# Fused attention and two feed-forward layers on one Trainium2 core: raw weights in ten places, 64x32 head tiles, a new layout of the first pass

## The chip, the cores and the metric

The kernel runs on one core of one Trainium2 chip. The metric is the device time of one execution in microseconds: the median of 3 runs is 771.13 us (770.52 to 771.54).

## The reference

```python
# attention: x is (4, 8, 512, 64), state is (4, 8, 32, 64), per batch and head, scale 1/8
a = softmax(scale * x @ state.T);      xread = a @ state      # rows of x read the state
a2 = softmax(scale * state @ x.T);     sread = a2 @ x         # the state reads x
t = concatenate([xread, sread], axis=2)    # then heads side by side: (2176, 512) tokens
h = t @ w_in                               # moe: 512 -> 2048
g = where(h >= 1, h, where(h <= -1, 0, (h + 1) ** 2 / 4))
t = g @ w_out                              # 2048 -> 512
h = t @ w_in2;  g = softplus(h);  out = g @ w_out2            # moe2, the same sizes
```

The weights are 64-bit floats; x, state and the output are 32-bit floats.

## The kernel before, in words

There are two phases. Phase 1 does attention and the first feed-forward layer for four tiles of 512 tokens (one batch each, the x tokens) and a small tile `s` of the 128 state tokens; phase 2 does the second layer over five tiles of 512 or 384 tokens. A tile is worked off in windows (16 of them, 4 for `s`), each for 128 of the 2048 hidden columns: 132 windows in all, in the loop `for i in range(NW + LAG + 1)`. In window `i` PE issues the first-layer products of window `i` (`l1`, 6 in phase 1) and the second-layer products of window `i - LAG` (`l2`, 12 in phase 1, three per block, as each operand is split into a high and a low fp32r part: `mm3`). Between them ACT opens the activation (`act_open`), DVE closes it (`close`), ACT copies the high part (`cut_hi`), and DVE (POOL in tile 0) subtracts the low part (`cut_lo`).

In phase 1 the read of the state is folded into the weights: for each batch `b` and pair `p` of 128-column blocks, `g_mm` (L404) multiplies the batch's state by the rebuilt weights `W1[p]` in four fp32 products of 256 columns. The stationary operand is `stb`, 64 columns wide, in which the two heads of a product stand block by block between zeros. `g_split` cuts the result into `gh` and `gl`; `l1` multiplies them by the transposed attention weights `ahi`, `alo`. `scores` (L213) uses `stb` in the same way with 512 columns of x. `Attn` holds the attention of one batch: names with `s_` belong to the softmax over x (its result `x1s` goes to tile `s`), names with `n_` to the softmax over the 32 states. `hops()` is a generator that does a few of these steps per window; `rest()` does the `s_` steps of batch 0 later.

The weights come as 64-bit floats (`w.bitcast(U32)`, two words each). A `Pair` is 1 MB of them: `load` issues the DMA on SP's queue into one of two buffers `ws`, `scale` (ACT, L107) and `conv` (DVE, L123 and L124) rebuild a 32-bit float, and `split` copies the high part (ACT) and subtracts the low part (POOL, L70, `wl<-cv,wh`). `pairs` is sorted by the window in which a pair is rebuilt; a load is issued when the pair two before it has been rebuilt, a `scale` one window ahead.

All instructions stand in the order in which the code issues them (`manual_schedule`): every engine works off its own queue in order, and so does SP with its DMAs. Ahead of the loop stands the start: state, pair 0 and x of batch 0 are loaded, x is transposed (L198), and the `n_` steps of batch 0 run through DVE and ACT until the first `l1` can go.

Of the kernel before, what the change touches and what calls it, by code (L numbers as in the profile page):

```python
# [18 lines left out]
def fused_kernel(ctx: ExitStack, tc: tile.TileContext, x, state, w1, w2, w3, w4, out):  # L19
# [10 lines left out]
    P = 128  # L30
# [12 lines left out]
    LAG = 3  # L43
    C2 = 2 * P
# [20 lines left out]

    def copy(dst, src):
        nc.scalar.activation(dst, src, AF.Copy)  # L67
# [7 lines left out]
    M = 2  # L75

# [3 lines left out]
    class Pair:  # L80
        def __init__(self, w, inward, p, dst, slots=None):
            self.w, self.inward, self.p, self.dst, self.slots = w, inward, p, dst, slots

        def load(self, tag=None, eng=None):
# [8 lines left out]
            if tag is None:  # L93
                self.raw = [new(base, shape, U32, "ws", 2)]
                nc.sync.dma_start(self.raw[0], src)
                return
            self.raw = [new(base, [P, 512 * M], U32, tag, 8) for _ in range(2)]
# [28 lines left out]
        def split(self):  # L126
# [3 lines left out]
            hi, lo = (new(pool, [P, 1024], F32R, t, n) for t in ("wh", "wl"))  # L130
            copy(hi, self.v)
            sub(nc.gpsimd, lo, self.v, f32(hi))
# [15 lines left out]
    stb = new(p1, [P, NJ, B, 2 * N], F32, "stb")  # L148
    nc.gpsimd.memset(stb, 0.0)
# [6 lines left out]
    def load_x(b, engs):  # L156
        xt[b] = new(at, [P, R, H, D], F32, f"x{(b + 1) // 2 % 2}")
        src = x[b].rearrange("h (p r) d -> r p h d", r=R)
        for r in range(R):
            engs[r % len(engs)].dma_start(xt[b][:, r], src[r])  # L160

    def warm(n):

        t = bank("l1", 2)
        for _ in range(n):
            nc.tensor.matmul(t[:, :P], ident, ident, start=True, stop=True)

    def load_state():
        st = new(at, [P, H, D], F32, "xT0")
        for b in range(B):  # L170
            eng = (nc.sync, nc.scalar)[b % 2]
            eng.dma_start(st[b * N : (b + 1) * N], state[b].rearrange("h n d -> n h d"))
        return st

    def place_state(st):
        ps = bank("at", 2).rearrange("p (j c) -> p j c", j=NJ)
        for j in range(NJ):
            nc.tensor.transpose(ps[:, j, :], st[:, 2 * j : 2 * j + 2, :].rearrange("p e d -> p (e d)"), ident)
        for e in range(2):
            sl = slice(e * D, (e + 1) * D)  # L180
            nc.vector.tensor_copy(
                stb[sl, :, :, e * N : (e + 1) * N], ps[sl].rearrange("p j (b n) -> p j b n", n=N)
            )
# [5 lines left out]
    class Attn:  # L189
# [6 lines left out]
        def x_transpose(self, j, ps, r):  # L196
            xb = xt[self.b]
            nc.tensor.transpose(  # L198
                ps[:, r * P : (r + 1) * P], xb[:, r, 2 * j : 2 * j + 2, :].rearrange("p e d -> p (e d)"), ident
            )  # L200
# [8 lines left out]
        def scores(self, g):  # L209
            self.ps[g] = bank("at", 2)  # L210
            for i in range(2):
                j = 2 * g + i
                nc.tensor.matmul(  # L213
                    self.ps[g][64 * i : 64 * i + 64, :], stb[:, j, self.b, :], self.xT[j], start=True, stop=True
                )

        def s_copy(self, g):
            self.e2[g] = new(base, [P, S], F32, "xs", 4) if self.b == 0 else new(at, [P, S], F32, f"xT{2 * g}")
            copy(self.e2[g], self.ps[g])

        def blocks(self, g, src=None):

            self.st[g] = new(at, [P, S], F32, "sa", 3)
            nc.vector.transpose(self.st[g], self.e2[g] if src is None else src)
# [17 lines left out]
        def s_turn(self, g):  # L242
            self.ps[g] = bank("at", 2)
# [13 lines left out]
        def s_read(self, js):  # L257
            xb = xt[self.b]
            if 0 in js:
                self.ps["s"] = bank("at", 2)  # L260
            for j in js:
                for r in range(R):
                    for e in range(2):
                        c0 = (2 * (j % 2) + e) * N
# [3 lines left out]
                            self.a2T[j // 2][:, r, c0 : c0 + N],  # L268
# [38 lines left out]
        def hops(self):  # L307

            for js in ((0, 1), (2,), (3,)):
                ps = [bank("at", 2) for _ in js]  # L310
                for j, t in zip(js, ps):
                    for r in range(R):
                        self.x_transpose(j, t, r)
                yield
                for j, t in zip(js, ps):
                    self.x_copy(j, t)
                yield
            self.scores(0)
            yield
            self.s_copy(0)  # L320
            yield
            self.scores(1)
            yield
            self.s_copy(1)
            self.blocks(0)
            self.s_max(0)
            yield
            yield
            self.s_exp(0)
            self.s_max(1)  # L330
            self.n_sub(0)
            self.blocks(1)
            yield
            yield
            self.s_exp(1)
            self.n_exp(0)
            self.s_norm(0)
            self.n_sub(1)
            yield
            self.s_turn(0)  # L340
            yield
            self.s_keep(0)
            self.s_norm(1)
            self.n_exp(1)
            self.n_norm(0)
            yield
            self.s_turn(1)
            yield
            self.s_keep(1)
            self.n_norm(1)  # L350
            self.n_back(0)
            yield
            self.s_read((0, 1))
            yield
            self.n_hi(0)
            if self.b < 3:
                self.n_lo(0)
            self.n_back(1)
            yield
            self.s_read((2, 3))  # L360
            yield
            self.n_hi(1)
            for g in range(NG):
                if self.b < 3 and g == 1 or self.b == 3 and g == 0:
                    self.n_lo(g)
            self.s_out()
            yield
            if self.b == 3:
                yield
                self.n_lo(1)  # L370
                yield

        def rest(self):
            yield
            for g in range(NG):
                self.s_max(g)
            yield
            yield
            for g in range(NG):
                self.s_exp(g)  # L380
            yield
            yield
            for g in range(NG):
                self.s_norm(g)
            yield
            for g in range(NG):
                self.s_turn(g)
                yield
                self.s_keep(g)
                yield  # L390
            self.s_read((0, 1, 2, 3))
            yield
            self.s_out()
            yield
# [11 lines left out]
    def g_split(b, p, ps):  # L406
        hi = new(p1, [P, NG * C2], F32R, "gh", 2)
        lo = new(p1, [P, NG * C2], F32R, "gl", 2)
        copy(hi, ps)
        sub(nc.vector, lo, ps, f32(hi))  # L410
        G[b, p] = [t.rearrange("p (g f) -> p g f", g=NG) for t in (hi, lo)]
# [14 lines left out]
    tiles2 = [units[0:4], units[4:8], units[8:11], units[11:14], units[16:17] + units[14:16]]  # L426
# [54 lines left out]
    def l1(w):  # L481
# [13 lines left out]
        elif w.ph == 1:  # L495
# [3 lines left out]
            terms = [(gh, ah, g) for g in range(NG)] + [(gh, al, g) for g in range(NG)] + [(gl, ah, g) for g in range(NG)]  # L499
# [31 lines left out]
    def evac(w):  # L531
        if w.ph == 1 and w.tl == "s":
# [3 lines left out]
            def pe():  # L536
                ps = bank("at", 2)
# [13 lines left out]
        for i in range(n):  # L551
            t = new(base, [P, 512], F32, "xs", 4)
            if i % 2 == 0:
# [54 lines left out]
    pairs = []  # L608
# [4 lines left out]
    for p in range(1, NP):  # L613
        plan_pair(Pair(w1, True, p, W1), 2 * (p - 1))
    for p in range(NP):
        plan_pair(Pair(w2, False, p, W2, lambda: pools["b"]), 2 * p + 1)
# [5 lines left out]
    pairs.sort(key=lambda t: t[0])  # L622
    for n, (a, pair) in enumerate(pairs):
        if n >= 3:
            b = pairs[n - 2][0]
            when(b + (b >= A0), "load", pair.load)
        if n >= 1:
            when(a - 1, "late", pair.scale)
        n = 2 if a >= A0 else 1
        for k in range(n):  # L630
# [3 lines left out]
    def plan_g(i, b, p):  # L634
        def pe():
            ps = bank("at", 2)
            g_mm(b, p, ps)
            return lambda: g_split(b, p, ps)
# [3 lines left out]
    for b, t0 in ((0, 0), (1, NF), (2, 2 * NF), (3, T3)):  # L642
        for p in range(NP):
            if (b, p) != (0, 0):
                plan_g(t0 + 2 * p - (1 if b == 0 else 2), b, p)
    gens = {}

    def plan_hops(i, make):


        def start():
            gens[i] = make()
# [3 lines left out]
    for b, i0, i1 in ((1, -1, 4), (2, NF - 1, NF + 5), (3, 2 * NF - 1, 2 * NF + 1)):  # L656
        when(i0, "load", lambda b=b: load_x(b, [nc.sync]))
        plan_hops(i1, lambda b=b: Attn(b).hops())
# [19 lines left out]
    with tc.manual_schedule():  # L678
# [106 lines left out]
```

## Time and profile before

| | us |
|---|---|
| median of 3 runs | 771.13 |
| the profiled execution | 772.06 |
| its span | 770.2 |
| PE busy | 743.0 (96%) |
| ACT busy | 458.3 (60%) |
| DVE busy | 437.3 (57%) |
| POOL busy | 103.7 (13%) |

The profile shows one execution. Busy times are sums over the span; a matmul's record lasts longer than its share of PE, since matmuls overlap, so the time from one start to the next is what it costs. A row's bracket says how long the engine sat idle ahead of it and what ended that. PEclk is the granted clock of TensorE as a share of 2.4 GHz.

### The profile page before, as it was taken

How to read it: one execution, taken by the hardware profiler on the slowest of the kernel's cores; microseconds unless marked ns; L12 is line 12 of the kernel's file. 1: busy time of each engine (PE TensorE's matmuls, PEld its weight loads, DVE VectorE, ACT ScalarE, POOL GpSimd, SP SyncE). 2: the span in 40 equal slices, each digit the busy share in tenths (PEclk: the TensorE clock that was granted, in tenths of full speed). 3: DMA queues.
4: the chain of work that ended last, by engine and by line, in shares of the span. 5: the costliest groups of instructions: out<-in, count | busy, mean ns of one | idle time of the engine just before them, and what ended most of it. 6: DMA issues, size and time to landing. Idle time of an engine off the chain costs nothing.

```text
span 770.2 us, 9775 instructions
## 1 busy us (share of the span) xinstructions
PE 743.0 (96%) x3768; PEld 606.3 (79%) x3768; DVE 437.3 (57%) x695; ACT 458.3 (60%) x800; POOL 103.7 (13%) x60
## 2 busy tenths in 40 slices
PE   5599899999999999999999999999999999999997
PEld 4366677867767788777888888888889998998986
DVE  4877964245337424555599984554654554555543
ACT  3677675445545435566778775655655666566563
POOL 0265670002000001122222320000000000000000
PEclk9799999999999999999999999999999999999999
DMA  9466363300010003144343400300020002001001
GB/s 289 110 217 217 109 194 81 55 1 1 1 55 1 1 1 110 56 128 159 110 164 110 164 0 1 96 1 1 0 89 9 1 0 83 1 1 41 1 1 41
DMA packets 39582, 52.00 MB, mean 68 GB/s; under 512 B 19312, under 2 KB 21872, under 8 KB 39536
## 3 DMA queue, kind: packets, MB, share of 16 engines
q1 hardware_dynamic: 36912, 50.73, 21.1%
q10 hardware_dynamic: 2624, 0.66, 0.4%
q8 instruction: 29, 0.48, 0.3%
q14 instruction: 17, 0.14, 0.1%
HBM read 42.47 MB, written 8.91 MB: 67 GB/s over the span
## 4 chain that ended last, share of the span: by engine, by line
PE 92%; DVE 4%; ACT 2%; DMA 1%; POOL 1%; issue 0%; SPq 0%; DVEq 0%; ACTq 0%
PE acc L441 16%; PE acc L442 16%; PE acc L443 16%; PE l L501 10%; PE l L443 8%; PE l L441 8%; PE l L442 8%; PE at L404 4%; PE l L488 2%; PE at L265 1%; PE at L213 1%; DMA wh<-in_moe_w_in_dram 1%; DVE w L124 1%; PE at L198 1%; DVE w L123 1%; POOL wl L70 0%
## 5 line engine op out<-in xcount | busy, mean ns | idle before, releaser
L70 DVE TENSOR_TENSOR gtl<-tl,gth 128x384 fp32r<-128x384 f32 (+1 forms) x80 | 48.9, 611 | 148.6 <-ACT gth L67 148.6
L577 ACT ACTIVATE ta<-l 128x384 f32<-128x384 f32 (+1 forms) x80 | 42.8, 535 | 128.7 <-PE l L443 128.7
L573 ACT ACTIVATE ta<-l 128x512 f32<-128x512 f32 x68 | 40.6, 598 | 128.2 <-PE l L501 104.3
L70 DVE TENSOR_TENSOR gtl<-ta,gth 128x512 fp32r<-128x512 f32 x52 | 36.0, 692 | 136.6 <-ACT gth L67 136.6
L442 PE MATMUL acc<-wl,gth 128*128 128x512 f32 x288 | 113.3, 393 | 0.0
L441 PE MATMUL acc<-wh,gth 128*128 128x512 f32 x288 | 113.2, 393 | 0.0
L443 PE MATMUL acc<-wh,gtl 128*128 128x512 f32 x288 | 112.7, 391 | 0.0
L441 PE MATMUL acc<-gth,wh 128*128 128x512 f32 x256 | 104.7, 409 | 0.0
L443 PE MATMUL acc<-gth,wl 128*128 128x512 f32 x256 | 100.2, 391 | 0.4 <-POOL wl L70 0.4
L442 PE MATMUL acc<-gtl,wh 128*128 128x512 f32 x256 | 100.3, 392 | 0.0
L70 POOL TENSOR_TENSOR wl<-cv,wh 128x1024 fp32r<-128x1024 f32 x24 | 62.8, 2615 | 220.8 <-ACT wh L67 219.5
L443 PE MATMUL l<-x,wl 128*128 128x384 f32 (+1 forms) x192 | 68.7, 358 | 0.0
L441 PE MATMUL l<-x,wh 128*128 128x384 f32 (+1 forms) x192 | 68.6, 357 | 0.0
L442 PE MATMUL l<-x,wh 128*128 128x384 f32 (+1 forms) x192 | 68.5, 357 | 0.0
L443 PEld LDWEIGHTS acc<-wh,gtl 128*128 128x128 f32 x288 | 54.1, 188 | 12.2
L441 PEld LDWEIGHTS acc<-gth,wh 128*128 128x128 f32 x256 | 48.1, 188 | 19.1 <-issue 9.1
L441 PEld LDWEIGHTS acc<-wh,gth 128*128 128x128 f32 x288 | 54.1, 188 | 11.2 <-issue 0.8
L442 PEld LDWEIGHTS acc<-wl,gth 128*128 128x128 f32 x288 | 54.0, 188 | 10.0
L443 PEld LDWEIGHTS acc<-gth,wl 128*128 128x128 f32 x256 | 48.1, 188 | 11.6 <-POOL wl L70 0.8
L70 DVE TENSOR_TENSOR tl<-tl,ta 128x384 f32<-128x384 f32 (+1 forms) x80 | 55.3, 691 | 2.8
L588 DVE SCALAR_TENSOR_TENSOR ta<-tb,ta 128x384 f32<-128x384 f32 (+1 forms) x80 | 55.9, 698 | 0.0
L442 PEld LDWEIGHTS acc<-gtl,wh 128*128 128x128 f32 x256 | 48.2, 188 | 8.8
(114 smaller groups left out, 1376.2 us busy)
## 6 DMA issues: line engine op xcount, KB each, us to landing
ws<-in_moe_w_out_dram SPq DMA_DIRECT2D x16, 1024.0 KB, 4.8
ws<-in_moe_w_in_dram SPq DMA_DIRECT2D x14, 1024.0 KB, 5.5
xd<-xs SPq DMA_DIRECT2D x16, 256.0 KB, 2.9
out_dram<-xs SPq DMA_DIRECT2D x16, 256.0 KB, 2.5
x<-in_x_dram SPq DMA_DIRECT2D x14, 256.0 KB, 6.2
xs<-xd SPq DMA_DIRECT2D x8, 256.0 KB, 6.3
wh<-in_moe_w_in_dram SPq DMA_DIRECT2D x2, 512.0 KB, 5.5
wl<-in_moe_w_in_dram SPq DMA_DIRECT2D x2, 512.0 KB, 7.7
```

The lines of the kernel that those rows point to most:

```text
L70: eng.tensor_tensor(dst, a, b, op=ALU.subtract)
L123: nc.vector.tensor_scalar(d, lo, 29, None, op0=ALU.logical_shift_right)
L124: nc.vector.scalar_tensor_tensor(d, hi, 3, d, op0=ALU.logical_shift_left, op1=ALU.bitwise_or)
L404: nc.tensor.matmul(o, stb[:, j, b, :], W1[p][:, j, :], start=True, stop=True)
L441: nc.tensor.matmul(o, lh, rh, start=first, stop=False)
L442: nc.tensor.matmul(o, lh, rl, start=False, stop=False)
L443: nc.tensor.matmul(o, ll, rh, start=False, stop=last)
L488: nc.tensor.matmul(w.h[:, i * P : (i + 1) * P], W1[f // 2][:, k, (f % 2) * P : (f % 2 + 1) * P], x1s[:, k, :], start=(k == 0), stop=(k == ...
L501: nc.tensor.matmul(w.h, l[:, g, f], r[:, g, :], start=i == 0, stop=i == len(terms) - 1)
L573: nc.scalar.activation(w.a, w.hc, AF.Relu, bias=1.0)
L577: nc.scalar.activation(w.a, w.hc, AF.Abs)
L588: nc.vector.scalar_tensor_tensor(w.a, w.b, 1.0, w.a, op0=ALU.subtract, op1=ALU.subtract)
```

## The change

- `stb` (zeros between the heads) goes; `stT` holds the transposed state without zeros, `stT0` that of batch 0. `heads` does `g_mm` and `scores` in eight products of 64 rows by 32 columns of the array, the two row halves into two PSUM banks of one lasting tile `side`, which also takes the place of the two rotating banks `at`. For batch 0, `scores0` does 16 products of 256 columns.
- The x of batch 0 is loaded in rows of 1 KB, in two DMAs on SP's queue behind pair 0; the state of batch 0 comes by itself, by ACT's queue, that of all batches later.
- The first ten pairs are loaded at once: besides the two buffers `ws`, the eight places of the split second-layer weights `wh0` to `wl7` take raw weights until their own are split. `A1` and `A2` say in which window a pair is rebuilt.
- The start also rebuilds pairs 1 of `w1` and 0 of `w2`, does `g_mm` of pair 1, and issues warm-up products between the steps.
- In the loop the order of the steps is a list (`ORDER`: windows 0 to 2, 3 to 15, the rest); `l2` follows two windows behind until window 14, three after. Attention of batch 1 does only its `n_` steps in tile 0, its `s_` steps (`rest`) start in window 17.
- The low parts of the weights and of tile 0's activations are subtracted by DVE instead of POOL. The order of the three terms in `l1` changes, the state tokens' tile stands elsewhere in `tiles2`, and the last output block is copied and stored in two halves.

```diff
+    LEAD = 14
+    ORDER = [
+        "l1 post hops evac open close l2 split early conv hi late hops lo pe load".split(),
+        "l1 post hops evac close l2 split early open conv hi late hops lo pe load".split(),
+        "l1 hops evac post close l2 split early hops open hi conv pe lo late load".split(),
+    ]
+    side = new(psum, [P, 2, 512], F32, "at")
...
             copy(hi, self.v)
-            sub(nc.gpsimd, lo, self.v, f32(hi))
+            sub(nc.vector, lo, self.v, f32(hi))
...
+    def scores0(xT):
...
+        for j in range(NJ):
+            for e in range(2):
+                for q in range(2):
...
+                    nc.tensor.matmul(
+                        side[j * N : (j + 1) * N, q, c], stT0[rows, h * N : (h + 1) * N], xT[j][rows, c], start=True, stop=True
+                    )
+    def heads(b, o, rhs):
+        for j in range(NJ):
+            for e in range(2):
+                rows = slice(e * D, (e + 1) * D)
+                if b == 0:
+                    s_h = stT0[rows, (2 * j + e) * N : (2 * j + e + 1) * N]
+                else:
+                    s_h = stT[rows, j, b * N : (b + 1) * N]
+                nc.tensor.matmul(o(e)[j * N : (j + 1) * N, :], s_h, rhs(j)[rows], start=True, stop=True)
...
-    def g_mm(b, p, ps):
-        for j in range(NJ):
-            i = j % 2
-            o = ps.rearrange("p (g f) -> p g f", g=NG)[64 * i : 64 * i + 64, j // 2, :]
-            nc.tensor.matmul(o, stb[:, j, b, :], W1[p][:, j, :], start=True, stop=True)
+    def g_mm(b, p, two=None):
+        o = (lambda e: side[:, e, :C2]) if two is None else (lambda e: two[e][:, :C2])
+        heads(b, o, lambda j: W1[p][:, j, :])
...
-            w.lo = nc.gpsimd if tl == 0 else nc.vector
+            w.lo = nc.vector
...
+    A1 = [-3, -2, 1, 3, 6, 6, 8, 12]
+    A2 = [-1, 2, 4, 4, 8, 10, 13, 15]
...
+    room = [(-9, None), (-9, None)] + [(-9, p) for p in range(NP)]
...
+    when(1, "pe", lambda: place_state(st))
+    when(1, "pe", lambda: warm(8))
+    for b, i0, i1 in ((1, -1, 3), (2, NF + 3, NF + 6), (3, 2 * NF - 1, 2 * NF + 1)):
         when(i0, "load", lambda b=b: load_x(b, [nc.sync]))
-        plan_hops(i1, lambda b=b: Attn(b).hops())
+        plan_hops(i1, lambda b=b: attn(b).head(), lambda b=b: aT0[b].reads(b > 1))
+    plan_hops(NF + 1, lambda: aT0[1].rest())
...
+        early[0].load()
+        load_x(0, [nc.sync])
+        for pair in early[1:3]:
+            pair.load()
         st = load_state()
+        for pair in early[3:]:
+            pair.load()
         warm(8)
+        place_state0(st0)
+        warm(8)
...
+        a0.scores()
+        warm(30)
+        run(-2, "early")
+        run(-2, "conv")
         for g in range(NG):
             a0.blocks(g, a0.ps[g])
...
+            k = i - LAG + (i < LEAD)
+            u = wins[k] if 0 <= k < NW and i != LEAD else None
```

## Rows read from the trace of the kernel before

**Rows 1.** The page, engines: busy us (share of the span) xinstructions.
```profile
PE 743.0 (96%) x3768; PEld 606.3 (79%) x3768; DVE 437.3 (57%) x695; ACT 458.3 (60%) x800; POOL 103.7 (13%) x60
```

**Rows 2.** Table by stretch: stretch, length, busy us of each engine, clock, DMA.
```profile
0.00:24.82 24.82, 10.79 (x53) 7.95 (x53) 13.43 (x24) 8.50 (x13) 2.64 (x8) 0.84 0.99 264
24.82:43.36 18.54, 13.78 (x52) 8.90 (x53) 14.35 (x18) 12.05 (x19) 6.89 (x4) 0.84 0.38 117
43.36:75.78 32.42, 32.42 (x157) 23.63 (x157) 24.62 (x28) 25.30 (x38) 19.13 (x10) 1.00 0.64 224
75.78:110.95 35.17, 31.81 (x206) 24.57 (x205) 31.74 (x42) 24.19 (x40) 24.32 (x15) 1.00 0.39 124
110.95:765.19 654.24, 654.20 (x3305) 541.23 (x3303) 353.20 (x588) 387.67 (x692) 50.72 (x25) 1.00 0.15 47
765.19:770.20 5.01, 0.00 (x0) 0.00 (x0) 0.01 (x1) 0.60 (x1) 0.00 (x0) 0.78 0.49 157
```

**Rows 3.** PE's timeline at the first windows: start us, us, operation [idle before <-releaser].
```profile
24.82 0.80 PE L501 MATMUL l<-ahi,gh 128*128 128x512 f32 x1 [8.02 <-ACT ahi L67]
...
43.36 0.73 PE L501 MATMUL l<-ahi,gh 128*128 128x512 f32 x2 [1.44 <-ACT gh L67]
```

**Rows 4.** PE's timeline around products with the state and of tile `s`.
```profile
112.40 1.08 PE L404 MATMUL at<-w,stb 128*64 128x256 f32 x8
113.41 0.50 PE L441 MATMUL acc<-gth,wh 128*128 128x512 f32 x1
...
160.78 1.08 PE L213 MATMUL at<-xT,stb 128*64 128x512 f32 x4
...
283.98 3.73 PE L488 MATMUL l<-x1s,w 128*128 128x128 f32 x32
287.47 0.48 PE L441 MATMUL acc<-gth,wh 128*128 128x512 f32 x1
```

**Rows 5.** All records of line 404 behind the first: count, min/median/max ns.
```profile
L404 PE MATMUL at<-w,stb x248: 379/379/431, 31.4 to 363.4; 128*64 128x256 f32 x124
```

**Rows 6.** Table by stretch, two of the loads' early stretches; last number GB/s.
```profile
12.00:14.00 2.00, 2.00 (x12) 2.00 (x12) 0.53 (x1) 0.00 (x0) 0.00 (x0) 0.58 1.08 399
...
22.00:24.00 2.00, 0.00 (x0) 0.00 (x0) 1.90 (x5) 0.38 (x1) 0.00 (x0) 0.50 1.11 180
```

**Rows 7.** DVE's timeline: start of the chain, a rebuilding, two long ones.
```profile
15.98 0.72 DVE L224 STREAM_TRANSPOSE sa<-at 128x512 f32<-128x512 f32 x1 [0.57 <-PE at L213]
...
27.41 0.42 DVE L123 TENSOR_SCALAR w<-wl 128x512 uint32<-128x512 uint32 x1
27.87 0.69 DVE L124 SCALAR_TENSOR_TENSOR w<-wl,w 128x512 uint32<-128x512 uint32 x1
28.48 0.42 DVE L123 TENSOR_SCALAR w<-wl 128x512 uint32<-128x512 uint32 x1
...
59.44 2.12 DVE L124 SCALAR_TENSOR_TENSOR cv<-ws,cv 128x1024 uint32<-128x1024 uint32 x1
...
70.53 1.22 DVE L124 SCALAR_TENSOR_TENSOR cv<-ws,cv 128x1024 uint32<-128x1024 uint32 x1
```

**Rows 8.** The chain that ended last, in order of time: start us, us, what.
```profile
127.63 0.44 PE at L245 x4
...
133.21 1.84 PE at L265 x64
...
139.36 0.87 PE at L198 x8
...
170.18 1.36 PE l L501 x6
...
174.25 1.36 PE l L501 x6
```

**Rows 9.** Groups by line and shape: busy us, mean ns, idle before.
```profile
L70 POOL TENSOR_TENSOR wl<-cv,wh 128x1024 fp32r<-128x1024 f32 x24 | 62.8, 2615 | 220.8 <-ACT wh L67 219.5 <-PE at L198 1.3
```

**Rows 10.** Timeline of the last copy.
```profile
765.19 0.60 ACT L67 ACTIVATE xs<-acc 128x512 f32<-128x512 f32 x1 [0.76 <-PE acc L443]
```

More of the change, by code (lines that the diff above doesn't have):

```diff
@@ L75, in fused_kernel @@
     M = 2
+    halves = [0]
     def flat(t):
@@ new lines, in scores0, with warm2 @@
+    def scores0(xT):
+        for j in range(NJ):
+            for e in range(2):
+                for q in range(2):
+                    rows = slice(q * D, (q + 1) * D)
+                    h = 2 * j + e
+                    c = slice(e * 256, (e + 1) * 256)
+                    nc.tensor.matmul(
+                        side[j * N : (j + 1) * N, q, c], stT0[rows, h * N : (h + 1) * N], xT[j][rows, c], start=True, stop=True
+                    )
+    def warm2(n):
+        for _ in range(n):
+            nc.tensor.matmul(side[:, 0, :P], ident, ident, start=True, stop=True)
@@ L305, in n_lo @@
             sub(eng or self.eng, self.alo[:, g, :], self.st[g], f32(self.ahi[:, g, :]))
[L307 to L371, printed above, removed]
@@ L373, in rest, with x_turn @@
-        def rest(self):
[L374 to L394, printed above, removed]
+        def x_turn(self, js):
+            for j in js:
+                self.ps["x", j] = at_bank()
+                for r in range(R):
+                    self.x_transpose(j, self.ps["x", j], r)
@@ L397, in fused_kernel, with both @@
+        def rest(self):
+            def both(f):
+                return lambda: [f(g) for g in range(NG)]
+            yield None, both(self.s_max)
+            yield None, both(self.s_exp)
+            yield None, both(self.s_norm)
+            yield both(self.s_turn), both(self.s_keep)
+            yield self.s_read, self.s_out
     W1 = [None] * NP
     G = {}
-    def g_mm(b, p, ps):
-        for j in range(NJ):
-            i = j % 2
-            o = ps.rearrange("p (g f) -> p g f", g=NG)[64 * i : 64 * i + 64, j // 2, :]
-            nc.tensor.matmul(o, stb[:, j, b, :], W1[p][:, j, :], start=True, stop=True)
@@ L414, in fused_kernel, with g_split @@
+    def g_split(b, p):
+        hi, lo = g_tiles(b, p)
+        copy(hi, side[:, :, :C2])
+        sub(nc.vector, lo, side[:, :, :C2], f32(hi))
     class Win:
@@ L552, in evac @@
             t = new(base, [P, 512], F32, "xs", 4)
+            if w is wins[-1] and i == n - 1:
+                b, r = tiles2[w.tl][i]
+                o = out[b * T : b * T + S, :].rearrange("(p r) d -> p r d", r=R)[:, r, :]
+                for c, eng in ((slice(0, 256), nc.sync), (slice(256, 512), nc.scalar)):
+                    if c.start:
+                        copy(t[:, c], acc[i][:, c])
+                    else:
+                        nc.vector.tensor_copy(t[:, c], acc[i][:, c])
+                    eng.dma_start(o[:, c], t[:, c])
+                break
             if i % 2 == 0:
@@ L709, in fused_kernel @@
             a0.n_exp(g)
-        early[0].scale()
+        g_mm(0, 1)
+        hi, lo = g_tiles(0, 1)
+        warm(14)
+        copy(hi, side[:, :, :C2])
         for g in range(NG):
-            a0.n_norm(g, nc.vector)
+            a0.n_norm(g, (nc.vector, nc.gpsimd)[g])
+        sub(nc.vector, lo, side[:, :, :C2], f32(hi))
         for g in range(NG):
@@ L715, in fused_kernel @@
             a0.n_hi(g)
+        for g in range(NG):
             a0.n_lo(g, nc.vector)
-        plan_hops(NF - 1, a0.rest)
+        run(-1, "early")
+        run(-1, "conv")
         run(-1, "load")
```

290 lines of the change are left out of this document (177 added, 113 removed).

## The prediction

> **What bounds the kernel now.** First the page's line of engines [rows 1]: PE is busy 96% of the span, DVE 57%, ACT 60%. That is a mean over unlike stretches, so next the table by stretch [rows 2]. From 110.95 us to the last matmul PE has 654.20 us of work in 654.24 us: there only a change in PE's own work moves the end. Before that it is another kernel. The first first-layer product starts at 24.82; from there to 43.36 PE works 13.78 of 18.54 us, from 75.78 to 110.95 31.81 of 35.17. Third, PE's timeline [rows 3]: the first product waited 8.02 us for ACT's `ahi`, and the one at 43.36 waited for `gh`, which ACT copies out of a product that needs a weight pair rebuilt on DVE. Fourth, DVE in those stretches [rows 2]: 31.74 busy of 35.17. So the start is bounded by DVE, everything after by PE. The waits there are DVE's time, not the ACT's that they name.
>
> I measure by one mark: the start of the seventeenth `l1`, the first of tile 1, at 110.95 us [rows 2].
>
> **The change, part by part.**
>
> *Small head tiles.* `g_mm` was four fp32 products of 256 columns, 128 rows by 64 columns of the array, half of the state operand zeros. It becomes eight of 64 by 32. First what one product costs: an fp32 product is two records, and 16 full-array products of 128 columns take 283.98 to 287.47 = 3.49 us, 0.218 each [rows 4]; 256 columns would be 0.436. Four in turn would be 1.74 us, but the block takes 112.40 to 113.41 = 1.01 us [rows 4], and two 512-column products (0.87 each) take 1.08 us with their end. So two products on different column halves run fully beside each other, both passes of each. If eight small tiles do the same, `g_mm` is one step of 0.44 us, plus what is over today: 1.01 - 2 x 0.436 = 0.14. Taken: 0.59, a saving of 0.42. No row shows 64-row tiles or more than two products side by side. From below the block can't go under 0.44; from above, eight in turn would be 3.5. If they overlap only in pairs, 4 x 0.436 + 0.14 = 1.88, a loss of 0.87; in fours, 1.01, no change. I take eight because what the rows show for two tiles (each tile goes on by itself, with its second pass not holding up the next tile's first) holds for eight if tiles are independent. There are 31 blocks behind the first (248 records, 8 to a block [rows 5]), of which 23 stand behind the mark (seven of batch 1, eight each of batches 2 and 3): 23 x 0.42 = 9.7 us, all on PE's path. `scores` of batches 2 and 3: two blocks of 1.0 us become one of 0.87 + 0.14; about 0.95 less each, 1.9 us.
>
> The Trainium skill, "TensorE: Matmul & The Clock Gate", Part 3 (the mechanism), says matmuls keep strict program order in start and end; the two passes of one product would then hold up the next tile, and eight products would be some nine half steps, about 2 us. The two-tile rows speak against it: in strict order two 512-column products need three steps of 0.436 = 1.31 us, and 1.08 was measured. "TensorEngine Tiling (Array Packing)", Key Properties, says the reverse, that tiles run independently; by that the block is the 0.59 above.
>
> *Start, up to the first product.* Removed: the zero fill of `stb`, x in small pieces on two queues. Added ahead of the first product: the state of batch 0 by itself, warm-up products, rebuilding of pair 1 (DVE) and `g_mm`/`g_split` of pair 1. Weights and x in large rows came at 399 GB/s, in 256-byte rows at 180 [rows 6]. x of batch 0 now comes in 1 KB rows right behind one weight pair: 2.2 MB from an assumed 2 us on, estimated at 300 to 400 GB/s, is there by 8 to 9.5 us. But ahead of the softmax chain DVE now has pair 1: two halves of 0.42 + 0.69 [rows 7], at their pitch (27.41 to 28.48) 1.07 each, 2.1 us. Walking the queues: pair 0 rebuilt by 8.8, products and transposes to 13, copies to 13.6, pair 1 on DVE to 16.6. So the chain starts near 16.5, against 15.98 [rows 7]. The chain itself (15.98 to 24.82) keeps its length: some 0.7 for `g_split`'s subtraction comes in, one multiplication goes to POOL. First product: 25.3, against 24.82; bounds 22 (DVE's pair 1 fits into the wait for the scores) and 28 (it doesn't fit, and x is late). No gain here, but pair 1 and its G are done, so that windows 0 to 3 have their operands.
>
> *First pass.* What is in it for PE in 16 windows: 16 `l1` of 1.36 and 13 `l2` of 2.71 (window 174.25 - 170.18 = 4.07 less 1.36) [rows 8]: 57.0. Further 7 g blocks of 0.65 with the change of mode (4.6), x transposes (16 in two steps of 0.87 [rows 8] with the change of tile, 2.0), scores of batch 1 (1.1), state (0.5): 65. Before, 8 blocks at 1.1, scores 2.1, turns of `e2` 2 x 0.44 and `s_read` 1.84 + 0.2 [rows 8] were in it too: 73, and 110.95 - 24.82 = 86.1 passed; 13 us were stalls and slow products.
> DVE: 13 pairs at 2.1 (27), 7 subtractions of 1024 columns now here instead of on POOL (L124's 1.22 of the same size [rows 7]: 8.5), 16 `close` and 16 `cut_lo` at the pitch of a 512-column instruction, 27.87 to 28.48 = 0.6 [rows 7] (19), 7 `g_split` (4.2), batch 1's column softmax (6), state (0.6): 66 us. Before it was busy 14.35 + 24.62 + 31.74 = 70.7 [rows 2], with `s_max`, `s_norm` in it. The move from POOL costs DVE some 18 us in this pass (8.5 + 16 x 0.6) and takes away the cause of its long instructions: L124 of 1024 columns took 2.12 at 59.44, a time in which POOL subtracted, and 1.22 at 70.53 with POOL idle [rows 7]; POOL's own subtraction took 2.6 in the mean [rows 9], twice as long.
> So PE has 65 and DVE 66, and what is left are waits between them. I walked windows 0 to 16 in ORDER's queue order: the first `l2` starts at 34.5 (waits for `cut_lo`, which waits for DVE's pairs 2 and 1 of the two weights), windows 4 and 9 lose 1.6 and 0.8 us, and the mark falls at 97.5. I add 1 us for hand-overs: 98.5; that leaves PE stalls of about 8. Bounds: 93 (stalls of 2.5) and 107 (the 13 us as before). Gain 12.4.
> What hides the rest: loads. Ten pairs and x are queued at once, 12.4 MB; at 399 GB/s they are there at 34, x of batch 1 (1 MB at 180 to 220) behind them at 39 to 40. It is needed at window 3's transposes, 39.3. If the mean is 300 GB/s, x is there at 50, and PE, which takes its work in order, stands 10 us with `l2` queued behind.
>
> *Moved.* `s_turn` and `s_read` of batch 1 (0.9 + 2.0) now stand behind the mark where PE is full: -2.9. Their DVE and ACT work goes to a stretch where DVE is busy 353 of 654 us.
>
> *POOL's later `wl` on DVE.* 17 subtractions of 1.2 behind the mark. Between weights and second layer DVE is fullest, but loses the same contention; PE has run 100% there. Taken 0, bound +3.
>
> *End.* The last copy (0.60 on ACT) and its store are halved over two engines and queues; from 765.19 to 770.2 it is 5.0 us [rows 10]. Taken -0.5, bounds 0 and -1.
>
> Sum: 12.4 - 2.9 + 9.7 + 1.9 + 0.5 = 21.6. The profiled execution: 772.06 with 770.2 of span; 750.5 after. The median of the runs, 771.13, lies 0.9 below: 749.6, said 750.
>
> **Rivals.**
> *A. Heads in fours.* No gain from tiles: 9.7 + 1.9 back, and some 1 us in the first pass: 763. For it: no row shows more than two. Against it: the two-tile rows show no sharing at all.
> *B. Order holds the tiles up (slower).* Only pairs overlap: each block 0.87 dearer, each `scores` 1.7 (8 x 0.436 + 0.14 = 3.6 against 2.0). Behind the mark 23 x 0.87 + 2 x 1.7 = 23.4; in the first pass 7 x 0.87 + 1.7 = 7.8, which eats the gain of 12.4 to 4.6. 771.1 - 4.6 + 2.9 + 23.4 - 0.5 = 792. It decides from about 1.34 us for a block on: without the heads the rest gives 12.4 - 2.9 + 0.5 = 10.0, which 30 blocks use up at 0.33 each.
> *C. The first pass stays bound.* Heads as forecast, but x of batch 1 comes late, or DVE's rebuilding in bursts (two pairs in windows 4, 6 and 8, 4.3 us each beside PE's 4.7) keeps the stalls: mark at 107, 758. For it: DVE at 66 against 65. Against it: loads had 399 GB/s where nothing held them.
> *D. It does more than that:* the mark at 93 and scores in one step: 744.
>
> **How the numbers follow.** Forecast 0.58 (744 to 756 with D's side in it), A 0.12, C 0.18, B 0.12. A and C are faster too. A measurement here tells 0.2%, 1.5 us, from no change. Faster 0.86, same 0.02 (only a mixture of B and the first pass's gain lands there), slower 0.12. The range leaves out B and a thin lower tail: 740 to 767.
>
> **What would show it.** Right: the rows of `g_mm` as 16 records within 0.55 to 0.7 us up to the next product, 23 of them behind the mark; the seventeenth `l1` near 98; no POOL beside L124, and L124 at its short length; PE without idle time from the mark on; clock 1.00 from 20 to 30 us, where the rows show 0.50 at 22 (1.2 of 2.4 GHz) after PE had stood for most of 8 us [rows 3, 6]. Wrong: blocks of over 1 us (A), of near 2 (B), a wait of the transposes for x, or of `l2` for `cut_lo` in windows 4 to 10 (C).

## The result, and the profile after

The changed kernel takes 753.5 us (median; 752.58 to 754.91) against 771.16 of the kernel before in the same session: ratio 0.9773 [0.9756 to 0.979]. The forecast was 750, with 740 to 767 as range. The profiled execution has 753.69 us and a span of 751.7 (772.06 and 770.2 before).

The page's line of engines, as in [rows 1]:

```profile
PE 742.1 (99%) x4216; PEld 610.2 (81%) x4216; DVE 442.9 (59%) x758; ACT 460.2 (61%) x811; POOL 17.6 (2%) x20
```

PE's busy time is nearly what it was; its idle time has fallen from 27.2 to 9.6 us, and POOL does next to nothing. The table by stretch, cut at the first first-layer product and at the mark, answers to [rows 2] (stretch, length, busy us of PE, PEld, DVE, ACT, POOL, clock, DMA, GB/s):

```profile
0.00:28.23 28.23, 25.30 (x225) 22.80 (x225) 14.63 (x30) 9.10 (x15) 2.79 (x8) 1.00 0.98 345
28.23:60.00 31.77, 29.59 (x179) 21.81 (x179) 28.83 (x48) 27.37 (x45) 0.00 (x0) 1.00 0.75 236
60.00:100.47 40.47, 40.47 (x239) 30.13 (x239) 37.08 (x60) 31.04 (x52) 7.63 (x6) 1.00 0.22 79
100.47:747.00 646.53, 645.99 (x3575) 535.26 (x3574) 361.30 (x621) 392.32 (x700) 7.22 (x6) 1.00 0.15 48
```

From 60 us to the last product PE is idle for 0.5 us only; before, its last stalls lay between 80 and 100 us. The mark lies at 100.47 (forecast 98.5, before 110.95): 10.5 us are won ahead of it, and 8.0 behind it (751.7 - 100.47 = 651.2 against 770.2 - 110.95 = 659.25). The first product comes at 28.23, *later* than before (24.82) and than the forecast (25.3).

PE's timeline of the changed kernel (start us, us, operation [idle before <-releaser]): the start, and blocks with the state:

```profile
6.71 1.03 PE L207 MATMUL at<-ident,cv 32*128 32x32 f32 x8 [1.57 <-DMA cv<-in_state_dram]
7.67 3.62 PE L195 MATMUL acc<-ident 128*128 128x128 f32 x16
11.23 0.66 PE L250 MATMUL l<-w,stT 64*32 64x256 f32 x16
11.82 2.05 PE L226 MATMUL at<-ident 128*128 128x128 f32 x16
13.71 1.91 PE L270 MATMUL acc<-ident,x 128*128 128x128 f32 x16
...
28.22 0.50 PE L546 MATMUL l<-ahi,gh 128*128 128x512 f32 x1
...
32.15 1.95 PE L195 MATMUL acc<-ident 128*128 128x128 f32 x16
...
37.85 0.50 PE L487 MATMUL acc<-gtl,wh 128*128 128x512 f32 x1 [0.98 <-DVE gtl L84]
...
40.58 0.66 PE L250 MATMUL at<-w,stT 64*32 64x256 f32 x16
41.17 0.74 PE L546 MATMUL l<-ahi,gh 128*128 128x512 f32 x2
...
53.85 1.09 PE L250 MATMUL at<-xT,stT 64*32 64x512 f32 x16
54.87 0.50 PE L486 MATMUL acc<-gth,wh 128*128 128x512 f32 x1
```

A block of eight small tiles, 40.58 to 41.17, takes 0.59 us, exactly the forecast, where four wide products took 1.01 [rows 4]. Of the block at 24.28 the records show how: eight of the 16 start within 46 ns, the other eight within 46 ns as well, 240 ns after the first. `scores` takes 1.02. That agrees with the tile rule weighed in the prediction (the Trainium skill, "TensorEngine Tiling (Array Packing)", Key Properties). The 2 us that the prediction worked out from strict order suppose that both passes of a product stand in the queue ahead of the next product; the records don't tell in which order the queue holds them, so the block's 0.59 us rules out the 2 us and not an order in start and end.

DVE's timeline shows why the start is late (same columns):

```profile
7.78 0.42 DVE L210 COPY stT<-at 128x256 f32<-128x256 f32 x1 [7.78 <-PE at L207]
8.12 0.42 DVE L139 TENSOR_SCALAR w<-wh 128x512 uint32<-128x512 uint32 x1
8.65 0.69 DVE L140 SCALAR_TENSOR_TENSOR w<-wh,w 128x512 uint32<-128x512 uint32 x1
9.26 0.42 DVE L139 TENSOR_SCALAR w<-wl 128x512 uint32<-128x512 uint32 x1
9.78 0.69 DVE L140 SCALAR_TENSOR_TENSOR w<-wl,w 128x512 uint32<-128x512 uint32 x1
14.78 0.69 DVE L277 COPY xT<-acc 128x512 f32<-128x512 f32 x1 [4.31 <-PE acc L270]
...
19.19 0.77 DVE L305 STREAM_TRANSPOSE sa<-at 128x256 f32<-128x256 f32 x2
```

The copy of the state stands ahead of the rebuilding of pair 0 and waits until 7.78 for the state's DMA, so pair 0 is done at 10.47 instead of 8.8. PE meanwhile does eight warm-up products, to 11.23, ahead of `g_mm`, and eight more ahead of the transposes. The first eight take 3.56 us (7.67 to 11.23), the second eight 1.89 (11.82 to 13.71): the first group runs at about half the pace, though the table's row has a clock of 1.00 for the whole start. The softmax chain starts at 19.19, not at 16.5, and from there to the first product takes 9.04 us, before 8.84 [rows 3, 7].

### The profile page after: what moved, and what is told of

It reads as the page before. It is cut to its first block, busy times and chain, and to the rows that moved or that the text cites. A ratio compares the mean times of both kernels' runs of the same rounds, so it can differ in the third digit from the quotient of the medians.

```text
span 751.7 us, 10616 instructions
## 1 busy us (share of the span) xinstructions
PE 742.1 (99%) x4216; PEld 610.2 (81%) x4216; DVE 442.9 (59%) x758; ACT 460.2 (61%) x811; POOL 17.6 (2%) x20
## 4 chain that ended last, share of the span: by engine, by line
PE 94%; DMA 5%; ACT 1%; DVE 0%; SPq 0%; issue 0%
PE acc L486 17%; PE acc L487 17%; PE acc L488 16%; PE l L546 12%; PE l L488 8%; PE l L486 8%; PE l L487 8%; PE at L250 3%; PE l L533 2%; DMA x<-in_x_dram 2%; DMA wl<-in_moe_w_out_dram 1%; DMA wh<-in_moe_w_in_dram 1%; PE at L345 1%; PE at L266 1%; DMA cv<-in_state_dram 1%; PE at L326 0%
## 5 line engine op out<-in xcount | busy, mean ns | idle before, releaser
L486 PE MATMUL acc<-gth,wh 128*128 128x512 f32 x256 | 102.0, 398 | 0.0
L84 DVE TENSOR_TENSOR gtl<-ta,gth 128x512 fp32r<-128x512 f32 x68 | 46.7, 686 | 42.0 <-ACT gth L81 42.0
L84 DVE TENSOR_TENSOR gl<-at,gh 128x512 fp32r<-128x512 f32 x31 | 21.3, 688 | 80.6 <-ACT gh L81 80.6
L486 PEld LDWEIGHTS acc<-wh,gth 128*128 128x128 f32 x288 | 54.1, 188 | 10.5
L487 PEld LDWEIGHTS acc<-gtl,wh 128*128 128x128 f32 x256 | 48.1, 188 | 11.3 <-DVE gtl L84 1.7
L84 DVE TENSOR_TENSOR tl<-tl,ta 128x384 f32<-128x384 f32 (+1 forms) x80 | 48.9, 612 | 2.8
L642 DVE SCALAR_TENSOR_TENSOR tl<-l,tl 128x384 f32<-128x384 f32 (+1 forms) x80 | 48.3, 604 | 0.0
```

The lines of the kernel that those rows point to most:

```text
L84: eng.tensor_tensor(dst, a, b, op=ALU.subtract)
L486: nc.tensor.matmul(o, lh, rh, start=first, stop=False)
L487: nc.tensor.matmul(o, lh, rl, start=False, stop=False)
L642: nc.vector.scalar_tensor_tensor(w.l, w.hc, 0.0, w.l, op0=ALU.max, op1=ALU.add)
```

## The experiments

Per profiled run: the first product, the mark, the pass between, and what is left of the span behind the mark (us); then the median and the ratio to before.

| kernel | first | mark | pass | behind | median | ratio |
|---|---|---|---|---|---|---|
| before | 24.82 | 110.95 | 86.1 | 659.3 | 771.16 | |
| after | 28.23 | 100.47 | 72.2 | 651.2 | 753.5 | 0.9773 [0.9756, 0.979] |
| e1 wide heads | 29.56 | 103.99 | 74.4 | 662.5 | 767.95 | 0.995 [0.9933, 0.9966] |
| e2 POOL subtracts | 27.87 | 107.47 | 79.6 | 651.2 | 760.87 | 0.9862 [0.9847, 0.9876] |
| e3 four places | 29.64 | 101.07 | 71.4 | 651.3 | 754.14 | 0.9774 [0.9759, 0.9788] |
| e4 steps back | 27.98 | 105.18 | 77.2 | 647.5 | 754.53 | 0.978 [0.9765, 0.9795] |
| b1 before, DVE subtracts | 23.37 | 111.88 | 88.5 | 659.3 | 772.91 | 1.0024 [1.0014, 1.0033] |
| e10 POOL, lag 3 | 28.17 | 107.94 | 79.8 | 651.3 | 761.68 | 0.9885 [0.9867, 0.9903] |
| e11 lag 3 | 27.14 | 103.68 | 76.5 | 651.3 | 756.54 | 0.9818 [0.98, 0.9837] |
| e12 POOL busy for nothing | 27.84 | 114.73 | 86.9 | 651.7 | 768.42 | 0.9965 [0.9952, 0.9977] |
| e6 start | 24.91 | 98.10 | 73.2 | 651.2 | 751.23 | 0.974 [0.9725, 0.9754] |
| e7 pair 1 later | 28.69 | 100.92 | 72.2 | 651.3 | 754.12 | 0.9779 [0.9764, 0.9793] |
| e8 both | 25.64 | 97.85 | 72.2 | 651.3 | 751.36 | 0.9741 [0.9727, 0.9756] |
| e9 start, warm | 24.59 | 97.59 | 73.0 | 651.2 | 751.1 | 0.974 [0.9726, 0.9755] |

In runs whose start is the same code, up to the order of the loads (e3) and a fill with zeros (e1), the first product falls anywhere from 27.1 to 29.6, so the pass and the part behind are better evidence than the mark.

**e1: heads of batches 1 to 3 as four wide products again.**

```diff
...
+        if b > 0:
+            for j in range(NJ):
+                i = j % 2
+                nc.tensor.matmul(o(j // 2)[64 * i : 64 * i + 64, :], stb[:, j, b, :], rhs(j), start=True, stop=True)
+            return
...
```

> The changed kernel with the products of batches 1 to 3 with the state done as before: four products of 128 rows by 64 columns with zeros between the heads, from a padded operand; batch 0 and all else as changed. Theory (eight small tiles run beside each other, PE's path): blocks back to 1.01 us from 0.59, scores back to about 2.0 from 1.02; behind the mark 23 x 0.42 + 2 x 0.9 = 11.5 us, in the first pass at most 1.3: 765 to 766.5 against 753.5. Rival (the heads are hidden, the first pass gave it all): 753.5 to 756.

PE's timeline of this kernel, a block behind the mark:

```profile
108.16 1.08 PE L251 MATMUL at<-w,stb 128*64 128x256 f32 x8
109.17 0.74 PE L553 MATMUL l<-ahi,gh 128*128 128x512 f32 x2
```

The block is at 1.01 again. Behind the mark the tiles are worth 11.3 us (11.6 forecast), in the pass 2.2 (at most 1.3 expected), and 1.3 lie in the start, where this kernel has the same products: 767.95 rather than 765 to 766.5, the theory's side by far.

**e2: POOL subtracts again (all weights, and tile 0's `cut_lo`).**

```diff
-            sub(nc.vector, lo, self.v, f32(hi))
+            sub(nc.gpsimd, lo, self.v, f32(hi))
...
-            w.lo = nc.vector
+            w.lo = nc.gpsimd if tl == 0 else nc.vector
```

> The changed kernel with the low parts of the weights and of tile 0's activations subtracted by POOL again. Theory (POOL beside DVE stretched the rebuilding and made the stalls of the first pass): long instructions of L140 return (2.1 us), the mark comes 6 to 10 us later, nothing changes behind it: 760 to 764. Rival (the ten places do it, the engine doesn't matter): 753 to 756. Third possibility (DVE is relieved of 18 us, which helps): under 753.

The time is in the theory's range, but all of its 7.4 us lie in the pass, and the reason is not the theory's alone. The table by stretch of this kernel:

```profile
27.87:107.47 79.60, 71.30 (x417) 51.56 (x417) 63.37 (x86) 58.81 (x96) 45.75 (x27) 1.00 0.42 136
```

PE stands for 8.3 us instead of 2.2, but DVE is busy for *less* than after (63.37 against 65.92). PE's waits from 24 to 112 us name POOL (releaser: us in total, times, longest):

```profile
PE acc L487 <- POOL gtl L84: 4.6, 4, 1.6
PE at L250 <- DVE gl L84: 1.4, 1, 1.4
PE at L266 <- DVE gl L84: 1.3, 1, 1.3
```

Groups by shape, 25 to 110 us, here (busy us, mean ns | idle before):

```profile
L84 POOL TENSOR_TENSOR gtl<-ta,gth 128x512 fp32r<-128x512 f32 x15 | 23.2, 1545 | 13.0 <-ACT gth L81 13.0
L140 DVE SCALAR_TENSOR_TENSOR w<-wh,w 128x512 uint32<-128x512 uint32 x4 | 6.1, 1533 | 2.4 <-ACT wh L123 2.3
L139 DVE TENSOR_SCALAR w<-wl 128x512 uint32<-128x512 uint32 x4 | 4.9, 1228 | 0.0
```

and in the changed kernel, 25 to 103 us:

```profile
L84 DVE TENSOR_TENSOR gtl<-ta,gth 128x512 fp32r<-128x512 f32 x15 | 10.3, 685 | 1.1 <-ACT gth L81 1.1
...
L84 DVE TENSOR_TENSOR wl<-cv,wh 128x1024 fp32r<-128x1024 f32 x7 | 8.5, 1220 | 1.1 <-ACT wh L81 1.1
...
L140 DVE SCALAR_TENSOR_TENSOR w<-wh,w 128x512 uint32<-128x512 uint32 x4 | 2.8, 694 | 0.4
...
L139 DVE TENSOR_SCALAR w<-wl 128x512 uint32<-128x512 uint32 x4 | 1.7, 422 | 0.0
```

Beside POOL, these two groups of DVE's rebuilding take more than twice as long. They are the ones that stretch most: others keep their length (`w<-wl,w` 693 ns in both), and all the rebuilding of the pass together takes 44 us instead of 31 (sums of the groups' durations). POOL's own subtraction takes 1545 ns against DVE's 685, with PE behind it.

**b1: the kernel before, with DVE subtracting and nothing else.** The edit is e2's first and last lines the other way round.

> The kernel before, with one edit of the change alone: DVE instead of POOL subtracts the low parts of the weights and of tile 0's activations. Theory (POOL beside DVE makes the stalls of the first pass; the trace of the changed kernel with POOL gave the mark 7 us later): the mark, 110.95 in the kernel before, comes 5 to 8 us earlier, 763 to 766.5. Rival (the old layout fills DVE with s steps as well, and 18 us more on it make it the bound): 771 to 778.

My theory was wrong: 772.91, nothing gained. The stretch between its first product and the mark, and a part of it:

```profile
23.37:111.88 88.51, 79.52 (x413) 58.17 (x413) 72.75 (x103) 61.67 (x95) 7.10 (x6) 0.95 0.48 159
...
39.07:42.48 3.41, 3.41 (x10) 2.66 (x9) 3.23 (x5) 1.37 (x3) 0.00 (x0) 0.50 0.95 303
```

DVE is busy for 72.75 us, before for 70.7 [rows 2]: for the pairs of `w2` (`cv`) L124's mean fell from 1787 to 1339 ns and L123's from 1340 to 746, and the subtractions that came in (11.4 and 9.1 us) used it up. But DVE's sum isn't all that holds this kernel back, for DVE stands idle for 15.8 of the 88.51 us. Lines of its timeline (ACT, ACT, DVE), and behind them the same load's scaling in the kernel before:

```profile
43.62 1.15 ACT L107 ACTIVATE ws<-ws 128x1024 f32<-128x1024 f32 x1 [3.18 <-DMA ws<-in_moe_w_in_dram]
44.65 1.05 ACT L67 ACTIVATE wh<-cv 128x1024 fp32r<-128x1024 f32 x1
45.73 1.23 DVE L70 TENSOR_TENSOR wl<-cv,wh 128x1024 fp32r<-128x1024 f32 x1 [3.33 <-ACT wh L67]
```

```profile
43.32 1.16 ACT L107 ACTIVATE ws<-ws 128x1024 f32<-128x1024 f32 x1
```

DVE waits for ACT's `wh` for 10.6 us in four such places, and ACT, which has the scaling of a later pair ahead of `wh` in its queue, waits for loads for 12.5 us (before: 3.0). And at 39 us, after PE had stood for 2.10 us, the granted clock is 0.50 for 3.4 us, where before it is 1.00; half of PE's 3.41 us of work there, 1.7 us by estimate, is about what b1 is slower by. So b1 shows that the move alone gains nothing in the old layout; whether DVE's sum, the loads into two buffers or the clock is the reason stays open.

**e12: DVE subtracts, and POOL does the same subtractions beside it into a tile that nobody reads.**

```diff
             sub(nc.vector, lo, self.v, f32(hi))
+            for h in (hi[:, :512], hi[:, 512:]):
+                sub(nc.gpsimd, idle, f32(h), f32(h))
...
+    idle = new(base, [P, S], F32, "idle")
...
+        if w.ph == 1 and w.tl == 0:
+            sub(nc.gpsimd, idle, f32(w.g[0]), f32(w.g[0]))
```

> The changed kernel, in which DVE goes on doing every subtraction of low parts, while POOL does subtractions of the same size at the same places beside it (high part minus itself, into a tile that nothing reads; a weight of 1024 columns as two of 512). So POOL is as busy beside DVE as in the kernel where it subtracts, but no engine waits for a result of it. Theory (contention is the price, as in the forecast's reason): DVE's instructions beside it stretch (L140 `w<-wh` from 694 toward 1533 ns), DVE has 66 us of first-pass work plus the stretch of 6 to 10, and the mark falls at 106 to 110 us: 759 to 763 us. Rival (the price is the later result and the queue on POOL, not its being busy): the mark stays within 1.5 us of 100.5 to 101: 753 to 755. Between the two, the share of the 7 us that returns is the share of contention.

Its table by stretch, the pass and what is behind the mark:

```profile
27.84:114.73 86.89, 73.97 (x417) 52.60 (x417) 81.92 (x106) 59.08 (x96) 47.67 (x34) 0.98 0.38 124
114.73:764.00 649.27, 646.79 (x3577) 535.50 (x3576) 379.46 (x624) 393.97 (x701) 59.44 (x42) 1.00 0.15 49
```

40.0 us more of POOL cost DVE 81.92 - 65.92 = 16.0 us in the pass, though no engine waits for POOL, and the pass is 14.7 us longer. So contention is real; I had put it at 6 to 10, too low. Some 1.4 us of the 14.7 are the clock (an estimate): from 38.7 to 42.1 it is 0.50 in this run, and half of PE's 2.85 us of work there would have gone at 1.00. Behind the mark DVE is also busy for 18.2 us more, and that costs 0.5: PE is the bound there. Of DVE's 16.0 us, 9.4 lie in its own subtractions (the changed kernel has 685 and 1220 ns for them):

```profile
L84 DVE TENSOR_TENSOR gtl<-ta,gth 128x512 fp32r<-128x512 f32 x14 | 15.1, 1076 | 0.0
L84 DVE TENSOR_TENSOR wl<-cv,wh 128x1024 fp32r<-128x1024 f32 x7 | 12.4, 1779 | 1.1 <-ACT wh L81 1.1
```

What the move does to DVE in the new layout, e2 tells: DVE's work without the subtractions is 65.92 - 10.3 - 8.5 = 47.1 us, and in e2, where POOL does them, DVE is busy for 63.37, 16.3 more. So the move puts 18.8 us on DVE and takes some 16 off it. That e12 also shows 16.0 is chance: there only some 6.6 us of it fall on the work that DVE has in e2 too, and why POOL stretches that work by 16 in e2 and by less here stays open.

**e10 and e11: the same two engines with a lag of 3 windows in the first pass (the change has 2 there).**

```diff
-    LEAD = 14
+    LEAD = 0
```

This is the whole edit of e11; e10 has e2's lines besides.

> The changed kernel with POOL's subtractions again, as in the run that gave the mark 107.5 and 760.9 us, and with l2 three windows behind l1 from the first window on (LEAD 0), not two. Theory (POOL's queue: with l2 two windows behind, its second product waits for POOL's gtl, which stands behind wl, sa and alo in POOL's order; contention between POOL and DVE is a small part): these waits go, the mark comes 3 to 6 us earlier than 107.5, 755 to 758. Rival (POOL stretches DVE's instructions, DVE's time is the bound): the mark stays at 106 to 108, 759.5 to 761.5.

> The changed kernel with l2 three windows behind l1 throughout (LEAD 0). Its only other difference from the kernel before it in this call is the engine of the subtractions. Theory (DVE does the low parts in time for either lag): the mark within 1.5 us of 100.5, 752.5 to 755. Rival (the shorter lag is what frees the first pass, as l2 has work earlier): 757 to 760.

In e10 PE no longer waits for POOL, but the time stays (the theory is wrong). PE's waits of e10, 24 to 112 us, and then those of e11:

```profile
PE at L250 <- DVE stT L238: 3.5, 1, 3.5
PE at L250 <- DVE w L140: 1.8, 2, 1.6
PE at L250 <- DVE gl L84: 1.0, 1, 1.0
```

```profile
PE at L266 <- DVE gl L84: 2.1, 1, 2.1
PE at L250 <- DVE stT L238: 1.8, 1, 1.8
PE l L546 <- DVE ta L639: 0.9, 1, 0.9
```

e11 alone is 3.0 us slower than after, between what theory and rival expected. But a longer lag isn't all that differs. Without an `l2` in window 2 PE stands for 3.5 us in e10 and twice for about 2 us in e11, and behind that the granted clock falls to 0.50, the lower of its two levels (1.2 of 2.4 GHz); in after and in e2 it is 1.00 all through the pass. The stretches, of e10 and of e11:

```profile
38.17:45.00 6.83, 5.52 (x30) 3.61 (x31) 6.45 (x11) 4.70 (x9) 2.57 (x2) 0.50 0.56 169
```

```profile
42.94:46.35 3.41, 3.41 (x10) 2.64 (x9) 3.20 (x7) 3.38 (x7) 0.00 (x0) 0.50 0.42 151
```

Half of PE's work in them, 2.8 us in e10 and 1.7 in e11, is an estimate of what the clock costs. POOL's subtracting costs the pass 7.4 us at lag 2 and 3.2 at lag 3, of which some 1.1 are then the clock. That the difference of the two is PE's wait for POOL's late result, and the rest DVE's own results that come late in bursts, is a reading of two pairs of runs; no run isolates it.

**e3: raw weights in four places.**

```diff
-    room = [(-9, None), (-9, None)] + [(-9, p) for p in range(NP)]
+    room = [(-9, None), (-9, None)] + [(-9, p) for p in (6, 7)]
...
+        run(-3, "load")
...
+        run(-2, "load")
```

> The changed kernel with four places for raw weights instead of ten (two buffers and two of the eight split places): four pairs loaded at once, each further load when a place comes free, two to four windows ahead. Theory (loads are not what bounds the first pass): 753 to 756, the mark within 2 us of 100.5. Rival (ten places free the first pass): waits of ACT's scaling for loads, the mark 6 to 10 us later, 760 to 764.

754.14: ten places rather than four are worth 0.6 us at most, within what can be told. With four places the loads are not what the first pass of the new layout waits for. No run has the new layout with the two buffers of the kernel before.

**e4: `s_turn` and `s_read` of batch 1 back in tile 0's pass.**

```diff
-        plan_hops(i1, lambda b=b: attn(b).head(), lambda b=b: aT0[b].reads(b > 1))
-    plan_hops(NF + 1, lambda: aT0[1].rest())
+        plan_hops(i1, lambda b=b: attn(b).head(), lambda b=b: aT0[b].reads(True))
```

> The changed kernel with batch 1's softmax over x and read of x (s steps) done in tile 0's pass again, as in the kernel before. Theory (PE has 2.8 us less behind the mark, the first pass takes 2.8 us of PE and some 3.5 of DVE more, and both are full there): mark +3 to +4, total 753.5 to 755.5. Rival (DVE is the narrow one in the first pass and its order of work breaks up: moving it was worth more than it cost): 757 to 760.

The pass grows by 5.0 and the part behind shrinks by 3.7; the mark is 4.7 later (3 to 4 expected), the median 1.0 up. The move is mostly work carried from one side of the mark to the other.

**e6: pair 0 rebuilt before the state is placed, eight warm-up products and those ahead of the transposes left out.**

```diff
-        place_state0(st0)
-        warm(8)
         run(-3, "early")
         run(-3, "conv")
+        place_state0(st0)
         two = [bank("l1", 2) for _ in range(NG)]
         g_mm(0, 0, two)
-        warm2(8)
```

> The changed kernel with another start: pair 0 is rebuilt ahead of the copy of batch 0's state on DVE, and the second group of 8 warm-up products and the 8 behind the first product with the state are left out. Theory (the first product was late, 28.2 us against 25.3 forecast, because these products stand in PE's queue ahead of work whose operands are there, and the state's copy ahead of the rebuilding): the transposes of x, now at 13.7 us, start by 10 to 11, the first l1 at 25 to 26, 750.5 to 751.5. Rival 1 (the warm-up products are needed: PE's clock falls to 0.5 as in the kernel before, at 20 to 30 us): no gain, 753 to 755. Rival 2 (DVE's sum of work bounds the first pass, an earlier start is given back in it): first l1 at 25 to 26 but the mark at 100, 753.

The first product comes 3.3 us earlier, the end 2.3. What it costs is in its table by stretch:

```profile
8.00:10.00 2.00, 1.77 (x20) 0.97 (x21) 0.17 (x1) 0.58 (x2) 0.00 (x0) 0.52 1.08 372
10.00:12.00 2.00, 2.00 (x13) 2.00 (x12) 0.69 (x1) 0.78 (x3) 0.00 (x0) 0.62 1.06 398
```

After PE had stood for 1.76 us (for the state) and 0.84 us, the granted clock is 0.52 and 0.62, mostly the lower of its two levels (1.2 of 2.4 GHz), and batch 0's transposes take 2.97 us instead of 1.84.

**e9: e6 with 16 warm-up products first and 4 behind the state.**

```diff
-        warm(8)
+        warm(16)
...
         place_state0(st0)
+        warm(4)
```

> The changed kernel with the start of the version that took 751.2 us (pair 0 rebuilt ahead of the copy of the state, two groups of warm-up products left out), and the first group of warm-up products 16 long instead of 8, with 4 behind the turned state. In that version the clock fell to 0.52 between 8 and 10 us after PE had stood from 5 to 6.7 us, and the transposes of x took 2.97 us against 1.84. Theory (the clock costs 1.5 us there and DVE's chain follows): clock 1.00 through 8 to 12 us, transposes back to 1.84, first l1 at 23 to 24, 749.3 to 750.3. Rival (x comes by DMA no earlier than it is used): transposes end as in that version, 751 to 751.7.

The same two stretches of this kernel:

```profile
8.00:10.00 2.00, 2.00 (x31) 1.44 (x29) 0.42 (x1) 0.00 (x0) 0.00 (x0) 1.00 1.07 373
10.00:12.00 2.00, 2.00 (x28) 1.83 (x24) 0.69 (x1) 1.57 (x4) 0.00 (x0) 1.00 1.05 396
```

The clock stays at 1.00 and the transposes take 1.90, yet the first product gains 0.3 us only, as the rival had it: the theory is wrong. From 12.0 to the first product DVE is busy for 11.46 of 12.59 us; that its chain sets the start is read from this. 751.1 is the lowest median, but e6's 751.23 lies within its spread (750.79 to 751.3).

**e7 and e8: pair 1's rebuilding behind the first softmax steps; e8 is e6 and e7 together, and `scores0` with its loops over j and e turned.**

```diff
-        run(-2, "early")
-        run(-2, "conv")
         for g in range(NG):
...
             a0.n_sub(g, (nc.vector, nc.gpsimd)[g])
+        run(-2, "early")
+        run(-2, "conv")
```

> The changed kernel with the rebuilding of pair 1 (2.2 us of DVE) moved behind the first steps of batch 0's softmax, from ahead of them. Theory (the chain on DVE from the scores to the first l1 is what sets the first l1): first l1 1 to 2 us earlier, 26.2 to 27.2. What it is worth at the mark: if the chain sets it, 751.5 to 752.5; if DVE's sum sets it (rival), 753 to 754, since the same rebuilding is then done later.

> Both of these edits together, and scores0 with its loops turned (column half outside, heads inside), so that each of the eight tiles gets its second product only when all have their first. Theory of the tiles (one product runs in a tile and one waits; tiles don't hold each other up before that): scores0 takes 1.0 to 1.1 us, 1.84 before. Rival (order makes no difference): 1.84. Time: 748 to 750 if the starts add up, 752 to 753.5 if DVE's sum gives them back.

e7 gains nothing, its theory is wrong: the rebuilding stays in the same queue of DVE, ahead of the later steps of the chain. e8 equals e6 within the spread, 751.36, between what theory and rival expected. `scores0` took 1.84 us in both orders, but in e8 the copies of x came in between its products, so whether their order matters is open.

## Why the prediction was right, and where it was not

*Small head tiles:* right in mechanism and size. Block 0.59 as forecast; `g_mm` and `scores` behind the mark give 11.1 us of PE's time (9.7 + 1.9 forecast), and e1 gives 11.3 back. Rivals A and B are out.

*The sum of DVE in the first pass:* 65.92 us measured, 66 forecast; pass 72.2, forecast 73.2. Two errors cancelled in the walk: PE's work was put at 65 and is 70.06 busy (eight warm-up products in window 1, 1.95 us, were overlooked, and `l1` takes 1.40, or 1.51 behind a block of small tiles, not 1.36), and the stalls at 8, of which the table shows 72.24 - 70.06 = 2.2. That the pass came out within 1.0 us is luck to that extent. Rival C (stalls stay) is out: x of batch 1 made no wait. The loads ahead of it are 11.9 MB (ten pairs, x of batch 0, the state), not 12.4, and SP issues the ten pairs between 0.7 and 23.3 us, not at once.

*"Takes away the cause of its long instructions":* that POOL's work stretches DVE's is shown by e12 (16.0 us for 40 us of POOL), and the step's 18 us of added work is 18.8. But the two nearly cancel (e2: 16.3 against 18.8), so it isn't a smaller sum of DVE that the move gains: moved alone in the old layout (b1) the subtractions gain nothing. In the new layout the move is worth 7.4 us. PE's waits for POOL's `gtl` (4.6 us in e2) point to how soon the low part is there; but in e10 these waits are gone and the time stays, so this is argued and not shown. So the 13.9 us by which the pass became shorter come from the layout and the move together; parts undone one at a time (heads 2.2, subtraction 7.4, steps of batch 1 5.0, short lag 4.3) need not add up, since each is taken from the full change. Some 2.4 of the 13.9 us are the clock (an estimate, half of the work named next): in the kernel before, 4.72 us of PE's work lie between 24.82 and 30.75 us at a granted clock of 0.50, in the changed kernel none.

*Moved steps:* 2.8 us more behind the mark in `s_turn` and `s_read`, forecast 2.9.

*Subtractions of POOL behind the mark:* taken as 0; e2 and after have the same 651.2.

*Start:* the step that failed. "Walking the queues: pair 0 rebuilt by 8.8, ... pair 1 on DVE to 16.6" left out that the state's copy stands ahead of pair 0 on DVE (done at 10.47, not 8.8) and the warm-up products ahead of `g_mm` on PE (to 11.23), so that the softmax chain starts 2.7 us later than forecast. 28.23 was just outside the bound of 28, and the end 3.5 us above the forecast is mostly this: e6, which puts the state's copy behind pair 0 and leaves these products out, has 24.91 and 751.23, 2.3 us less. The clock at 20 to 30 us is 1.00, as forecast.

*Behind the mark:* 8.0 won, 9.2 forecast. Not forecast: from start to start the `l1` take 1.9 us more and the `l2` 0.6 less. In the 1.9 are a wait of 0.5 for `gl` ahead of batch 1's `s_read`, the only one that the waits list behind the mark, and the step from small tiles to the full array, which now comes ahead of `l1` (1.51 against 1.40). The end gave 1.1 (5.5 us from the last product's start to the end of the span before, 4.4 now) where 0.5 was taken.

## What to carry to other kernels

Small products that leave rows of the array to zeros are worth cutting into tiles that fill it, once two tiles in a trace are seen to run fully beside each other. Work moved from a helper engine that slows its neighbour down to that neighbour may leave the neighbour's sum nearly as it was; here it paid in one layout (7.4 us) and not in the other, so price the time at which the result is there, and what else that engine's queue waits for, as well as the sum. When two runs are compared, look at the granted clock of the same stretch in both: e10, e11, e12 and b1 differ from their partners in it too. In a walk along queues, write down every instruction ahead of the first needed one, warm-up products and copies that wait for a DMA included.

## What the runs showed of the hardware that was not expected

Of the 16 records of eight fp32 products of 64x32 tiles with 256 columns, eight start within 46 ns of each other and the other eight 240 ns later. 40 us of POOL subtractions beside DVE lengthen DVE's work by 16 us although no engine waits for one of them (e12), 9.4 of them in DVE's own subtractions. The six products of an `l1` take 1.51 us from start to start behind a block of small tiles (62.56 to 64.07) and 1.40 without one (66.79 to 68.19).
